# Attention plus gated layer on one core: the mask tables of the opening built in fewer steps, and the check of the two counts moved behind the last minimum

## The chip, the cores and the metric

The kernel runs on one core of a Trainium2 chip. The metric is device time in microseconds (us) of one execution. Engines are named as in the profile: PE multiplies matrices, PEld loads its weights, DVE, ACT and POOL work on vectors, SP issues most transfers; ACT can issue transfers too, in a queue of its own.

## The reference

Four batches of eight heads, 768 positions, head size 64. A query sees a key if the key is one of the first `n_global` (8) positions or lies 0 to `n_local`-1 (95) positions behind it. The two counts are inputs (int64), so the mask is made on the chip. The attention's output goes through a gated layer with 512 inputs and 1536 hidden units.

```
rel = pos[:, None] - pos[None, :]
is_global = pos[None, :] < int(n_global)
is_local = (rel >= 0) & (rel < int(n_local))
keep = is_global | is_local
dist = where(is_global & ~is_local, n_local, abs(rel))
scores = scale * q @ k.T - slopes[h] * dist        # kept places
scores = where(keep, scores, -1e9)
a = exp(scores - max); a = a / (sum(a) + 1e-9); x = a @ v
out = (sigmoid(x @ w_gate) * (x @ w_val)) @ w_out
```

## The kernel before

The tokens are cut into 8 blocks of 384 (three tiles of 128). A block's attention goes by pairs of heads: four pairs, three tiles each. A tile's window has 256 keys: 96 before it, 32 slots for the global keys, and its own 128. For a tile the kernel computes scores on PE (L368), adds a distance table and takes the row's minimum on DVE (L401, `tensor_tensor_reduce`), the exponential on ACT (L414), transposes on PE (L447), and the product with v on PE (L497). The gated layer follows with 12 slices of hidden units (L559 into the layer, L599 out of it).

Block 0's attention runs alone, as an opening; from then on the attention of a block is woven into the gated layer of the block before. During block 0 the weights, which arrive as 64-bit numbers, are also rebuilt as pairs of 32-bit halves (L193 and L200 on ACT, L209 on DVE, L230 on ACT, L181 on POOL).

The opening needs the distance tables. `n_local` and `n_global` come as two transfers on SP's queue (L77), ahead of the queries and keys (L296, L304, L305). DVE makes 32-bit floats of their low and high words and joins them (`nf`, L81 to L84); `build_tables` (L109) forms distances (`dist` for 256 keys, `dist0` for the 128 keys of a sequence's first tile) from index ramps that POOL writes (L113 to L117), and `build_pair` (L152) scales them by a head's slope: on DVE for the first pair, on POOL for the other three. `tab` are the 256-wide tables, `tabs` the 128-wide ones for first tiles.

The tables hold only for counts within bounds (`n_local` 1 to 97, `n_global` 0 to 32). The kernel tests that, and whether a row had no key at all, in one `flag` (L758 to L768): four comparisons of `nf`, one of the largest minimum. At the end every engine loads the flag (L844) and branches (L845): flag 0 ends the program, flag 1 runs a general version of the whole (not run with these inputs). The program's end also waits for the last stores of the output (`ost` to `out`, L625 on SP, L619 on ACT).

A scheduler orders the instructions of each engine; `issue_after` only adds an order between two of them. Within an engine they run in that order. The pools of the main part are closed at L748 (`inner.close()`); the pool `gpool`, opened after that (L750), lies on their memory, among it that of `ost`, so a tile in it may be written only when whoever used that memory before is done.

Of the kernel before, what the change touches and what calls it, by code (L numbers as in the profile page):

```python
# [16 lines left out]
ALU = mybir.AluOpType  # L17
# [3 lines left out]
P = 128  # L21
PREV = 96
GLOB = 32
SLOT = GLOB + P
WIN = PREV + SLOT
NEG = 1.0e30


@with_exitstack
def attn_moe_kernel(ctx, tc, qT, kT, v, n_global, n_local, wg, wv, wo, out, B, H, S, D):  # L30
    nc = tc.nc
    DM = H * D
    NC = DM // P
# [23 lines left out]
    spool = inner.enter_context(tc.tile_pool(name="spool", bufs=2))  # L57
# [5 lines left out]
    def issue_after(later, earlier):  # L63
        tc.add_manual_dep(
            later.ins,
            earlier.ins.name,
            mybir.DependencyInfo(mybir.DependencyClass.NoSync, mybir.DependencyReason.DATA),
            reason="issue order",
        )


    nf = cpool.tile([P, 2], F32, name="nf")


    words = cpool.tile([P, 2, 2], I32, name="words")
    for k, src in enumerate((n_local, n_global)):
        nc.sync.dma_start(  # L77
            words[:, k], src.bitcast(I32)[0:2].rearrange("(a b) -> a b", a=1).to_broadcast([P, 2])
        )
    wf = cpool.tile([P, 3, 2], F32, name="wf")  # L80
    nc.vector.tensor_copy(wf[:, 0:2].rearrange("p w k -> p k w"), words)  # L81
    nc.vector.tensor_scalar(wf[:, 2], wf[:, 0], 0.0, None, op0=ALU.is_lt)
    nc.vector.tensor_tensor(wf[:, 2], wf[:, 2], wf[:, 1], op=ALU.add)
    nc.vector.scalar_tensor_tensor(nf, wf[:, 2], 2.0 ** 32, wf[:, 0], op0=ALU.mult, op1=ALU.add)  # L84
    ident = cpool.tile([P, P], F32, name="ident")
    warm = cpool.tile([P, 1], F32, name="warm")
    nc.vector.memset(warm, 0.0)
# [18 lines left out]
    tabs = [cpool.tile([P, WIN], BF16, name=f"tab{h}") for h in range(H)]  # L106
    tabs0 = [cpool.tile([P, P], BF16, name=f"tabs{h}") for h in range(H)]
    nms = cpool.tile([P, 2 * (B * NTB * NPAIR)], F32, name="nms")
    def build_tables():  # L109

        nl, ng = nf[:, 0:1], nf[:, 1:2]
        reli = spool.tile([P, WIN], I32, name="pT", tag="pT", bufs=PTB)
        nc.gpsimd.iota(reli[:, 0:PREV], pattern=[[-1, PREV]], base=PREV, channel_multiplier=1)  # L113
        nc.gpsimd.iota(reli[:, PREV:PREV + GLOB], pattern=[[1, GLOB]], base=0, channel_multiplier=0)
        nc.gpsimd.iota(reli[:, PREV + GLOB:WIN], pattern=[[-1, P]], base=0, channel_multiplier=1)
        coli = mpool.tile([P, P], I32, name="work", tag="work", bufs=WORKB)
        nc.gpsimd.iota(coli, pattern=[[1, P]], base=0, channel_multiplier=0)  # L117
        rel = spool.tile([P, WIN], F32, name="pT", tag="pT", bufs=PTB)
        nc.vector.tensor_copy(rel, reli)
        col = mpool.tile([P, 2, P], F32, name="work", tag="work", bufs=WORKB)  # L120
        nc.vector.tensor_copy(col[:, 0], coli)
        loc = spool.tile([P, WIN], F32, name="pT", tag="pT", bufs=PTB)
        pen = mpool.tile([P, 2, P], F32, name="work", tag="work", bufs=WORKB)
        cur = slice(PREV + GLOB, WIN)
        kg, only, both = col[:, 0], col[:, 1], pen[:, 0]
        nc.vector.tensor_scalar(loc, rel, 0.0, None, op0=ALU.is_ge)
        nc.vector.tensor_scalar(kg, kg, ng, None, op0=ALU.is_lt)
        nc.vector.scalar_tensor_tensor(loc, rel, nl, loc, op0=ALU.is_lt, op1=ALU.mult)
        nc.vector.tensor_tensor(rel, rel, loc, op=ALU.mult)
        dist = wraw.tile([P, WIN], BF16, name="dist", bufs=1)  # L130
        dist0 = wraw.tile([P, P], BF16, name="dist0", bufs=1)

        nc.vector.tensor_tensor(only, kg, loc[:, cur], op=ALU.is_gt)
        nc.vector.tensor_tensor(both, kg, loc[:, cur], op=ALU.max)
        nc.vector.scalar_tensor_tensor(only, only, nl, rel[:, cur], op0=ALU.mult, op1=ALU.add)
        nc.vector.tensor_scalar(both, both, 1.0, NEG, op0=ALU.subtract, op1=ALU.mult)
        nc.vector.tensor_tensor(dist0, both, only, op=ALU.subtract)
        build_pair(0, True, (dist, dist0))

        gsl = slice(PREV, PREV + GLOB)  # L140
        nc.vector.tensor_copy(loc[:, gsl], kg[:, 0:GLOB])
        nc.vector.tensor_scalar(rel[:, gsl], kg[:, 0:GLOB], nl, None, op0=ALU.mult)
        nc.vector.tensor_scalar(loc, loc, 1.0, NEG, op0=ALU.subtract, op1=ALU.mult)
        nc.vector.tensor_tensor(dist, loc, rel, op=ALU.subtract)
        return dist, dist0

    built = set()
    last_min = []
# [3 lines left out]
    def build_pair(s, zero, dist):  # L152
        if (s, zero) in built:
            return
        built.add((s, zero))
        for h in (2 * s, 2 * s + 1):
            eng = nc.gpsimd if s else nc.vector
            eng.tensor_scalar((tabs0 if zero else tabs)[h], dist[zero], slopes[h] / SCALE, None, op0=ALU.mult)


    w1h = [wpool.tile([P, 2, NC, P], F32R, name=f"w1h{f}") for f in range(NF)]
# [192 lines left out]
    def scores(bi, s, t):  # L354
# [542 lines left out]
```

## Time and profile before

| | us |
|---|---|
| median of three runs | 739.73 (738.4 to 740.57) |
| the profiled execution | 739.84 |
| its span, first to last instruction | 738.1 |
| PE busy in the span | 722.8 (98%) |
| DVE, ACT, POOL busy | 474.7, 410.8, 228.2 |

All times in the sections below are from the start of that span. A row of the timeline gives start, duration, engine, line of the code, operation, what it writes and reads, and in brackets how long the engine had been idle and what ended that. Rows of engines with a q (SPq, ACTq, DVEq) are what an engine's sequencer does: issuing a transfer, loading a flag, branching, waiting for a semaphore.

### The profile page before, as it was taken

What the parts mean: (1) busy time and instruction counts of PE and PEld (TensorE: products, weight loads), DVE (VectorE), ACT (ScalarE), POOL (GpSimd) and SP (SyncE); (2) the same over time, 40 slices, a digit from 0 to 9 for tenths busy, and PEclk for the clock granted to TensorE, in tenths of its full rate; (3) what the DMA queues carried; (4) which work ended last, traced back from release to release, by engine and by line L of the source; (5) the groups of instructions that cost most, each with busy time, mean ns of one, the idle gap of its engine ahead of it and who ended that gap; (6) DMA issues with size and microseconds to landing.
All of it is one profiled execution on the core that took longest, in us unless ns stands there. A gap on an engine that the chain in (4) does not pass through costs nothing. (4 is left out here: it accounts for less than half of the span.)

```text
span 738.1 us, 12514 instructions
## 1 busy us (share of the span) xinstructions
PE 722.8 (98%) x4403; PEld 655.9 (89%) x4403; DVE 474.7 (64%) x1279; ACT 410.8 (56%) x938; POOL 228.2 (31%) x238
## 2 busy tenths in 40 slices
PE   8999999999999999999999999999999999999996
PEld 5758788989889999999999999999999999999995
DVE  6765577577877877776777777666787867321111
ACT  4787686656555555565456655555555664332222
POOL 5437366323222323232232323213232231221222
PEclk8999999999999999999999999999999999999999
DMA  8688573524455342442435442353435234010001
GB/s 256 182 256 273 175 211 101 134 56 88 101 89 152 83 110 68 91 113 58 87 84 112 118 102 69 52 133 75 96 78 112 72 44 86 16 44 1 1 0 46
DMA packets 136868, 74.28 MB, mean 101 GB/s; under 512 B 87136, under 2 KB 129120, under 8 KB 136800
## 3 DMA queue, kind: packets, MB, share of 16 engines
q1 hardware_dynamic: 136656, 73.17, 40.0%
q8 instruction: 36, 0.59, 0.4%
q14 instruction: 32, 0.26, 0.1%
q10 hardware_dynamic: 144, 0.26, 0.1%
HBM read 49.81 MB, written 6.29 MB: 76 GB/s over the span
## 5 line engine op out<-in xcount | busy, mean ns | idle before, releaser
L181 POOL TENSOR_TENSOR w2l<-w2f,w2h 128x512 fp32r<-128x512 f32 x89 | 120.3, 1351 | 361.9 <-ACT w2h L212 354.8
L559 PE MATMUL ps_g<-xh,w1l 128*128 128x384 f32 x384 | 132.1, 344 | 1.1 <-ACT work L567 1.1
L559 PE MATMUL ps_u<-xh,w1l 128*128 128x384 f32 x384 | 130.8, 341 | 0.1
L559 PE MATMUL ps_g<-xl,w1h 128*128 128x384 f32 x384 | 129.6, 338 | 0.2 <-DVE xl L540 0.2
L559 PE MATMUL ps_g<-xh,w1h 128*128 128x384 f32 x384 | 129.6, 337 | 0.0
L559 PE MATMUL ps_u<-xl,w1h 128*128 128x384 f32 x384 | 129.3, 337 | 0.0
L559 PE MATMUL ps_u<-xh,w1h 128*128 128x384 f32 x384 | 129.1, 336 | 0.0
L576 DVE SCALAR_TENSOR_TENSOR work<-work,ps_u 128x384 f32<-128x384 f32 x90 | 49.7, 552 | 123.4 <-PE ps_u L559 122.6
L579 ACT ACTIVATE hh<-work 128x384 fp32r<-128x384 f32 x90 | 46.9, 521 | 128.4 <-DVE work L576 128.3
L414 ACT ACTIVATE work<-work,nms 128x256 f32<-128x256 f32 (+1 forms) x192 | 92.0, 480 | 30.0 <-DVE nms L401 29.5
L599 PE MATMUL ps_o<-w2l,hh 128*128 128x512 f32 x267 | 104.7, 392 | 1.8 <-POOL w2l L181 1.8
L599 PE MATMUL ps_o<-w2h,hh 128*128 128x512 f32 x267 | 104.1, 390 | 0.0
L599 PE MATMUL ps_o<-w2h,hl 128*128 128x512 f32 x267 | 103.6, 389 | 0.0
L181 DVE TENSOR_TENSOR hl<-work,hh 128x384 fp32r<-128x384 f32 x90 | 78.8, 875 | 25.4 <-ACT hh L579 25.3
L212 ACT ACTIVATE w2h<-w2f 128x512 fp32r<-128x512 f32 x89 | 56.0, 630 | 55.1 <-PE ps_o L599 54.3
L559 PEld LDWEIGHTS ps_g<-xh,w1l 128*128 128x128 f32 x384 | 72.3, 188 | 5.3 <-issue 2.1
L559 PEld LDWEIGHTS ps_u<-xh,w1l 128*128 128x128 f32 x384 | 72.1, 188 | 4.0 <-issue 1.0
L559 PEld LDWEIGHTS ps_g<-xl,w1h 128*128 128x128 f32 x384 | 72.2, 188 | 2.8 <-issue 1.0
L559 PEld LDWEIGHTS ps_u<-xl,w1h 128*128 128x128 f32 x384 | 72.2, 188 | 1.0
L559 PEld LDWEIGHTS ps_g<-xh,w1h 128*128 128x128 f32 x384 | 72.2, 188 | 0.6 <-issue 0.3
L462 DVE COPY halves<-work 128x512 int16<-128x512 int16 (+1 forms) x144 | 62.8, 478 | 15.0 <-DMA turned<-halves 13.4
L559 PEld LDWEIGHTS ps_u<-xh,w1h 128*128 128x128 f32 x384 | 72.2, 188 | 0.0
(131 smaller groups left out, 1160.6 us busy)
## 6 DMA issues: line engine op xcount, KB each, us to landing
qr<-in_qT SPq DMA_DIRECT2D x56, 192.0 KB, 3.4
kr<-in_kT SPq DMA_DIRECT2D x32, 192.0 KB, 2.7
v<-in_v SPq DMA_DIRECT2D x32, 192.0 KB, 3.4
raw<-in_w_gate SPq DMA_DIRECT2D x12, 512.0 KB, 5.2
raw<-in_w_val SPq DMA_DIRECT2D x12, 512.0 KB, 6.1
raw<-in_w_out SPq DMA_DIRECT2D x12, 512.0 KB, 3.8
out<-ost SPq DMA_DIRECT2D x23, 256.0 KB, 2.1
v<-in_v SPq DMA_DIRECT2D x16, 144.0 KB, 3.7
```

What stands on the lines that cost most here:

```text
L181: eng.tensor_tensor(out, a, b, op=ALU.subtract)
L212: ins = nc.scalar.activation(hi, w, AF.Copy)
L414: ins = nc.scalar.activation(sb[:, j, :w], sb[:, j, :w], AF.Exp, scale=-1.0, bias=nm[:, j:j + 1], accum_out=sm[:, j:j + 1])
L462: nc.vector.tensor_copy(dst, words[:, :, :, h])
L559: nc.tensor.matmul(ps[:, :n], wt[f][:, i, c], xt[:, c, :n], start=(k == 0), stop=(k == 3 * NC - 1))
L576: nc.vector.scalar_tensor_tensor(a[:, :n], a[:, :n], 1.0, pss[1][:, :n], op0=ALU.add, op1=ALU.mult)
L579: nc.scalar.activation(hh[:, :n], a[:, :n], AF.Copy)
L599: ins = nc.tensor.matmul(outs[bi][t], ht[:, t * P:(t + 1) * P], wt, start=(f == 0 and k == 0), stop=(f == NF - 1 and k == len(parts) - 1),)
```

## The change

The two counts are joined into one array (`counts`, the host stacks them as they are), and one transfer on ACT's queue brings them. The tables are made from the low words alone (`low`): the ramps are written so that one product gives a huge number where a place is ruled out, and maxima and minima combine them, straight from the integers. The sign of the slope moves into the scaling. The join of low and high words, with the four comparisons that use it, moves behind the main loop, into `gpool`, and is placed in order behind the last minimum. Lines of the new kernel have other numbers; L139 is its L158, L382 its L401, L831 its L844.

```
-    for k, src in enumerate((n_local, n_global)):
-        nc.sync.dma_start(
-            words[:, k], src.bitcast(I32)[0:2].rearrange("(a b) -> a b", a=1).to_broadcast([P, 2])
-        )
-    wf = cpool.tile([P, 3, 2], F32, name="wf")
-    nc.vector.tensor_copy(wf[:, 0:2].rearrange("p w k -> p k w"), words)
-    nc.vector.tensor_scalar(wf[:, 2], wf[:, 0], 0.0, None, op0=ALU.is_lt)
-    nc.vector.tensor_tensor(wf[:, 2], wf[:, 2], wf[:, 1], op=ALU.add)
-    nc.vector.scalar_tensor_tensor(nf, wf[:, 2], 2.0 ** 32, wf[:, 0], op0=ALU.mult, op1=ALU.add)
+    nc.scalar.dma_start(words.rearrange("p k w -> p (k w)"), counts.bitcast(I32).rearrange("(a b) -> a b", a=1).to_broadcast([P, 4]))
+    low = cpool.tile([P, 2], F32, name="low")
...
+        nc.vector.tensor_scalar(off, reli, 0.0, NEG, op0=ALU.is_lt, op1=ALU.mult)
+        nc.vector.tensor_tensor(rel, reli, off, op=ALU.max)
+        nc.vector.tensor_copy(low, words[:, :, 0])
...
+        nc.vector.tensor_scalar(off, rel, nl, NEG, op0=ALU.is_ge, op1=ALU.mult)
+        nc.vector.tensor_scalar(dist0, col, ng, NEG, op0=ALU.is_ge, op1=ALU.mult)
+        nc.vector.tensor_tensor(dist, rel, off, op=ALU.max)
+        nc.vector.tensor_scalar(dist0, dist0, nl, None, op0=ALU.max)
+        nc.vector.tensor_copy(dist[:, gsl], dist0[:, 0:GLOB])
+        nc.vector.tensor_tensor(dist0, dist0, dist[:, cur], op=ALU.min)
         build_pair(0, True, (dist, dist0))
...
-            eng.tensor_scalar((tabs0 if zero else tabs)[h], dist[zero], slopes[h] / SCALE, None, op0=ALU.mult)
+            eng.tensor_scalar((tabs0 if zero else tabs)[h], dist[zero], -slopes[h] / SCALE, None, op0=ALU.mult)
...
     late["pool"] = gpool
+    nf = gpool.tile([P, 2], F32, name="nf")
+    wf = gpool.tile([P, 3, 2], F32, name="wf")
+    issue_after(nc.vector.tensor_copy(wf[:, 0:2].rearrange("p w k -> p k w"), words), last_min[-1])
+    nc.vector.tensor_scalar(wf[:, 2], wf[:, 0], 0.0, None, op0=ALU.is_lt)
+    nc.vector.tensor_tensor(wf[:, 2], wf[:, 2], wf[:, 1], op=ALU.add)
+    nc.vector.scalar_tensor_tensor(nf, wf[:, 2], 2.0 ** 32, wf[:, 0], op0=ALU.mult, op1=ALU.add)
```

The places where the order moves follow. First DVE in the opening. Before, from the arrival of `words` to the first minimum's tables:

```order
L81 CAST wf<-words 128x2x2
L82 TENSOR_SCALAR wf<-wf 128x2
L83 TENSOR_TENSOR wf<-wf 128x2
L84 SCALAR_TENSOR_TENSOR nf<-wf 128x2
L127 TENSOR_SCALAR work<-work,nf 128x128
L128 SCALAR_TENSOR_TENSOR pT<-pT,nf 128x256
L766 TENSOR_SCALAR top<-nf 1x1 x4
...
L137 TENSOR_TENSOR dist_216<-work 128x128
L144 TENSOR_TENSOR dist<-pT 128x256
L158 TENSOR_SCALAR tabs_129<-dist_216 128x128
```

Now, on DVE, from `low` on (two steps, L114 and L115, stand ahead and need no count):

```order
L116 CAST low<-words 128x2
L119 TENSOR_SCALAR work<-work,low 128x256
L120 TENSOR_SCALAR dist_204<-work,low 128x128
L121 TENSOR_TENSOR dist<-work 128x256
L122 TENSOR_SCALAR dist_204<-dist_204,low 128x128
L123 COPY dist<-dist_204 128x32
L124 TENSOR_TENSOR dist_204<-dist_204,dist 128x128
L139 TENSOR_SCALAR tab_115<-dist 128x256
L139 TENSOR_SCALAR tab_116<-dist 128x256
L139 TENSOR_SCALAR tabs_123<-dist_204 128x128
L139 TENSOR_SCALAR tabs_124<-dist_204 128x128
```

Between the arrival of the counts and the first table there were twenty instructions; now there are seven.

Second, POOL's tables for the other three pairs. Before (`tabs_131` and `tabs_132` are the first-tile tables of pair 1, `tab_123` and on the wide ones):

```order
L158 TENSOR_SCALAR tabs_131<-dist_216 128x128
L158 TENSOR_SCALAR tabs_132<-dist_216 128x128
...
L158 TENSOR_SCALAR tabs_136<-dist_216 128x128
L158 TENSOR_SCALAR tab_123<-dist 128x256
L158 TENSOR_SCALAR tab_124<-dist 128x256
```

Now, on POOL (`tab_117` is the wide table of pair 1's first head, `tabs_125` its first-tile table):

```order
L139 TENSOR_SCALAR tab_117<-dist 128x256
L139 TENSOR_SCALAR tab_118<-dist 128x256
...
L139 TENSOR_SCALAR tab_121<-dist 128x256
L139 TENSOR_SCALAR tabs_125<-dist_204 128x128
L139 TENSOR_SCALAR tabs_126<-dist_204 128x128
```

Five wide tables now stand ahead of the first-tile table that pair 1 needs first.

Third, DVE at the end of the program, with what each instruction waits for. Before, behind the last minimum's blocks (the flag was complete some 25 rows earlier, at L768):

```order
L622 TENSOR_SCALAR ost<-ps_o_7680 128x512 [waits DMAHW1_49,DMAHW0_49,PE_49]
L617 TENSOR_SCALAR ost<-ps_o_7681 128x256 [waits DMAHW2_49,PE_49]
L844 TENSOR_LOAD flag [waits DVE_49]
L845 COMPARE_AND_BRANCH
```

Now, on DVE, the same place (`DMAHW` are semaphores of transfers; the values waited for on 2, 3 and 4 are those that the last three stores of `ost` set, `DMAHW4` being ACT's, the very last):

```order
L598 TENSOR_SCALAR ost<-ps_o_7666 128x256 [waits DMAHW1_49,PE_49]
L735 CAST wf<-words 128x2x2 [waits DMAHW3_49,DMAHW4_49,DMAHW2_49,DMAHW7_49,Activation_49,Pool_49]
L736 TENSOR_SCALAR wf<-wf 128x2 [waits DVE_49]
L737 TENSOR_TENSOR wf<-wf 128x2 [waits DVE_49]
L738 SCALAR_TENSOR_TENSOR nf<-wf 128x2 [waits DVE_49]
L753 TENSOR_SCALAR top<-nf 1x1 [waits DVE_49]
L753 TENSOR_SCALAR top<-nf 1x1 x3
L755 TENSOR_REDUCE flag<-top 1x1 [waits DVE_49]
L831 TENSOR_LOAD flag [waits DVE_49]
L832 COMPARE_AND_BRANCH
```

Nine instructions moved from the opening and from the main loop to behind the last store, and the flag's load on all engines stands behind them.

## Rows read from the trace of the kernel before

**Rows 1.** The page: busy time of PE, PEld, DVE, ACT and POOL.

```profile
PE 722.8 (98%) x4403; PEld 655.9 (89%) x4403; DVE 474.7 (64%) x1279; ACT 410.8 (56%) x938; POOL 228.2 (31%) x238
```

**Rows 2.** Windows: length, busy of PE, PEld, DVE, ACT, POOL, clock, DMA share, GB/s.

```profile
11.00:21.00 10.00, 10.00 (x55) 6.56 (x51) 5.14 (x19) 8.10 (x24) 5.92 (x8) 0.51 0.88 313
...
22.00:30.00 8.00, 7.71 (x74) 4.96 (x73) 6.37 (x30) 5.24 (x21) 6.05 (x12) 1.00 0.85 259
...
40.00:100.00 60.00, 59.21 (x319) 43.96 (x318) 38.27 (x100) 45.69 (x96) 27.93 (x57) 1.00 0.75 232
100.00:728.00 628.00, 624.12 (x3805) 582.99 (x3805) 408.87 (x1074) 340.36 (x775) 180.37 (x141) 1.00 0.35 80
```

**Rows 3.** Timeline of DVE, opening.

```profile
4.77 0.17 DVE L81 CAST wf<-words 128x4 f32<-128x4 int32 x1 [2.37 <-DMA words<-in_n_global]
...
5.57 0.29 DVE L127 TENSOR_SCALAR work<-work,nf 128x128 f32<-128x128 f32 x1
...
6.17 0.32 DVE L766 TENSOR_SCALAR top<-nf 1x1 f32<-1x1 f32 x4
...
8.18 0.41 DVE L144 TENSOR_TENSOR dist<-pT 128x256 bf16<-128x256 f32 x1
8.52 0.40 DVE L158 TENSOR_SCALAR tabs<-dist 128x128 bf16<-128x128 bf16 x2
...
9.12 0.27 DVE L401 CUSTOM_DVE_ANT_0 work<-ps_s,tabs 128x128 f32<-128x128 f32 x1
```

**Rows 4.** Timeline of SP, opening: issues of transfers.

```profile
0.85 0.39 SPq L77 DMA_DIRECT2D words<-in_n_local  x1
...
1.76 0.43 SPq L296 DMA_DIRECT2D qr<-in_qT  x1
```

**Rows 5.** Transfers issued from 0 to 9 us: count, KB each, us to landing.

```profile
words<-in_n_local SPq DMA_DIRECT2D x1, 1.0 KB, 2.6
words<-in_n_global SPq DMA_DIRECT2D x1, 1.0 KB, 3.4
```

**Rows 6.** Timeline of PE, opening.

```profile
6.17 0.34 PE L368 MATMUL ps_g<-kr,qr 64*128 64x128 f32 x1 [1.12 <-DMA kr<-in_kT]
...
9.66 0.48 PE L368 MATMUL ps_g<-kr,qr 64*128 64x256 f32 x1 [1.48 <-DVE nms L401]
...
10.66 0.37 PE L368 MATMUL ps_o<-kr,qr 64*128 64x128 f32 x1
...
21.48 0.37 PE L368 MATMUL ps_g<-kr,qr 64*128 64x128 f32 x1
...
27.05 0.37 PE L368 MATMUL ps_o<-kr,qr 64*128 64x128 f32 x1
```

**Rows 7.** Timeline of ACT, opening.

```profile
14.55 1.10 ACT L193 ACTIVATE bits<-raw 128x1024 int32<-128x1024 uint32 x1
15.55 1.11 ACT L200 ACTIVATE top<-raw 128x1024 f16<-128x1024 bf16 x1
...
20.05 1.06 ACT L230 ACTIVATE w1h<-bits 128x1024 fp32r<-128x1024 f32 x1
...
22.36 0.40 ACT L414 ACTIVATE work<-work,nms 128x128 f32<-128x128 f32 x1 [1.25 <-DVE nms L401]
```

**Rows 8.** Timeline of POOL, tables of pairs 1 to 3.

```profile
8.34 3.66 POOL L158 TENSOR_SCALAR tabs<-dist 128x128 bf16<-128x128 bf16 x6 [6.26 <-DVE dist L137]
12.08 5.14 POOL L158 TENSOR_SCALAR tab<-dist 128x256 bf16<-128x256 bf16 x6
```

**Rows 9.** Line L845, SP waiting for stores: count, ns min/median/max, first to last.

```profile
L845 SPq EVENT_SEMAPHORE  x8: 17/17/17, 733.6 to 736.7; - x8
```

**Rows 10.** Line L768, the flag's reduction: count, ns min/median/max, first to last.

```profile
L768 DVE TENSOR_REDUCE flag<-top x1: 147/147/147, 655.8 to 655.8; 1x1 int32<-1x5 f32 x1
```

**Rows 11.** The chain that ended last: its end (start, us, what).

```profile
732.65 0.37 DVEq L844
...
733.74 0.06 DVE top L846
```

More of the change, by code (lines that the diff above doesn't have):

```diff
@@ L29, in attn_moe_kernel @@
 @with_exitstack
-def attn_moe_kernel(ctx, tc, qT, kT, v, n_global, n_local, wg, wv, wo, out, B, H, S, D):
+def attn_moe_kernel(ctx, tc, qT, kT, v, counts, wg, wv, wo, out, B, H, S, D):
     nc = tc.nc
@@ L69, in issue_after @@
         )
-    nf = cpool.tile([P, 2], F32, name="nf")
     words = cpool.tile([P, 2, 2], I32, name="words")
-    for k, src in enumerate((n_local, n_global)):
-        nc.sync.dma_start(
-            words[:, k], src.bitcast(I32)[0:2].rearrange("(a b) -> a b", a=1).to_broadcast([P, 2])
-        )
-    wf = cpool.tile([P, 3, 2], F32, name="wf")
-    nc.vector.tensor_copy(wf[:, 0:2].rearrange("p w k -> p k w"), words)
-    nc.vector.tensor_scalar(wf[:, 2], wf[:, 0], 0.0, None, op0=ALU.is_lt)
-    nc.vector.tensor_tensor(wf[:, 2], wf[:, 2], wf[:, 1], op=ALU.add)
-    nc.vector.scalar_tensor_tensor(nf, wf[:, 2], 2.0 ** 32, wf[:, 0], op0=ALU.mult, op1=ALU.add)
+    nc.scalar.dma_start(words.rearrange("p k w -> p (k w)"), counts.bitcast(I32).rearrange("(a b) -> a b", a=1).to_broadcast([P, 4]))
+    low = cpool.tile([P, 2], F32, name="low")
     ident = cpool.tile([P, P], F32, name="ident")
@@ L109, in build_tables @@
     def build_tables():
-        nl, ng = nf[:, 0:1], nf[:, 1:2]
+        nl, ng = low[:, 0:1], low[:, 1:2]
+        cur, gsl = slice(PREV + GLOB, WIN), slice(PREV, PREV + GLOB)
         reli = spool.tile([P, WIN], I32, name="pT", tag="pT", bufs=PTB)
         nc.gpsimd.iota(reli[:, 0:PREV], pattern=[[-1, PREV]], base=PREV, channel_multiplier=1)
-        nc.gpsimd.iota(reli[:, PREV:PREV + GLOB], pattern=[[1, GLOB]], base=0, channel_multiplier=0)
-        nc.gpsimd.iota(reli[:, PREV + GLOB:WIN], pattern=[[-1, P]], base=0, channel_multiplier=1)
@@ L116, in build_tables @@
[L116 to L129, printed above, removed]
+        nc.gpsimd.iota(reli[:, gsl], pattern=[[0, GLOB]], base=-1, channel_multiplier=0)
+        nc.gpsimd.iota(reli[:, cur], pattern=[[-1, P]], base=0, channel_multiplier=1)
@@ L130, in build_tables @@
+        col = mpool.tile([P, P], I32, name="work", tag="work", bufs=WORKB)
+        nc.gpsimd.iota(col, pattern=[[1, P]], base=0, channel_multiplier=0)
+        far = mpool.tile([P, 2, WIN], F32, name="work", tag="work", bufs=WORKB)
+        rel, off = far[:, 0], far[:, 1]
+        nc.vector.tensor_scalar(off, reli, 0.0, NEG, op0=ALU.is_lt, op1=ALU.mult)
+        nc.vector.tensor_tensor(rel, reli, off, op=ALU.max)
+        nc.vector.tensor_copy(low, words[:, :, 0])
         dist = wraw.tile([P, WIN], BF16, name="dist", bufs=1)
@@ L131, in build_tables @@
         dist0 = wraw.tile([P, P], BF16, name="dist0", bufs=1)
[L133 to L137, printed above, removed]
-        build_pair(0, True, (dist, dist0))
-        gsl = slice(PREV, PREV + GLOB)
@@ L141, in build_tables @@
[L141 to L144, printed above, removed]
+        nc.vector.tensor_scalar(off, rel, nl, NEG, op0=ALU.is_ge, op1=ALU.mult)
+        nc.vector.tensor_scalar(dist0, col, ng, NEG, op0=ALU.is_ge, op1=ALU.mult)
+        nc.vector.tensor_tensor(dist, rel, off, op=ALU.max)
@@ L880 @@
         "v": _np.ascontiguousarray(v.transpose(0, 2, 1, 3)).reshape(B * S, H * D),
-        "n_global": _np.asarray(inputs["n_global"]).reshape(1),
-        "n_local": _np.asarray(inputs["n_local"]).reshape(1),
+        "counts": _np.stack([inputs["n_local"], inputs["n_global"]]),
         "w_gate": _slices(inputs["moe_w_gate"]),
```

## The prediction, made before the changed kernel ran

> **What bounds the kernel now.** I read the page first: PE is busy 722.8 of 738.1 us [rows 1]. Then the windows: from 100 to 728 us PE lacks only 3.9 us of being always busy, from 40 to 100 us only 0.8 [rows 2]. So most of the run is PE's own work, which the change leaves alone; it can win or lose only at the two ends, and what the opening gains arrives at the end as long as the stretch from 40 to 100 us can follow.
>
> In the opening PE waits. It starts on the scores at 6.17, when the keys land, and is stopped again for 1.48 us until 9.66 by the first minima [rows 6]. DVE meanwhile waits 2.37 us for the second list of counts, starts at 4.77 and builds tables until the first minimum at 9.12 [rows 3]. Behind that the granted clock is at its lower level (0.51 over 11 to 21, so 1.2 GHz); PE is called busy all ten microseconds, and pair 2 starts at 21.48. At the upper level (2.4 GHz) pair 2 takes 27.05 - 21.48 = 5.6 us, while pair 1, begun at 10.66, held PE 10.8 us before pair 2's start [rows 2, 6].
>
> At the end DVE's last instruction is at 733.74, but SP waits for the stores until 736.7, and the span closes at 738.1: 1.4 us of leaving behind the last store [rows 9, 11].
>
> **The opening, step by step.** *Counts.* The one transfer is issued by ACT at about 0.8, as SP's first was at 0.85, and lands 2.6 to 3.4 us later [rows 4, 5]: DVE starts on it at 3.5 to 4.3, I take 3.9. SP loses two issues, so queries and keys go out 1.76 - 0.85 = 0.9 us sooner, and the first scores can start at 5.3 [rows 4, 6].
>
> *Tables.* Four tiny dependent steps took 5.57 - 4.77 = 0.8, so 0.2 each; four comparisons that don't depend on each other 0.32; a dependent product of two 256-wide tiles 0.34 (8.18 to 8.52); the four scalings 0.60 (8.52 to 9.12) [rows 3]. The new chain: `low` 0.2, the two threshold steps 0.4, the 256-wide maximum 0.34, a 128-wide maximum 0.2, the copy 0.2, the minimum 0.2, the scalings 0.6: 2.1 in place of 9.12 - 4.77 = 4.35. The two steps ahead of `low` run while DVE sat idle. No row has an operation from integers to a 16-bit table; if each of the seven cost as much as the 256-wide product's 0.4 us, the chain were 3.4, if all were tiny 2.0. The first minimum then stands at 6.0 (5.5 to 7.7): 3.1 us sooner, held back neither by the scores (5.3 plus half a microsecond) nor by the exponential table that ACT now loads 0.4 us later.
>
> *What is late next.* PE had work until its stop, 9.66 - 1.48 = 8.2 [rows 6]; begun 0.9 sooner that ends at 7.3, when the minima of the first tile are done. The third tile's scores start there rather than at 9.66 (2.4 us sooner), and the stop is gone. POOL now writes five wide tables ahead of pair 1's first-tile table: five by 5.14 / 6 = 0.86 and one by 0.61 [rows 8] from about 5.3 make 10.2, where DVE wants it at about 10. That costs 0.2 us, up to 1 if POOL starts late.
>
> *The raw weights.* ACT's L193 needs weights that SP issues only 0.9 us sooner: 14.55 becomes about 13.5. In the new order ACT does L193 and L200 (2.1 from the first's start to the second's end), a copy and pair 1's last two exponentials (0.4 to 0.5 each; the narrower exponential took 0.40) and L230 (1.1), and only then pair 2's first exponential [rows 7]: 13.5 + 2.1 + 1.3 + 1.1 = 18.0, where before it was at 22.36. That is 4.4 us, if PE is at the upper clock level; if PE falls to the lower level as before, it sets the pace and the gain stays at the 3.1 of the first minimum.
>
> On the clock the rows show the lower level from about 11 us on, behind the stop of 1.48 us, and that pairs 2 and 3 held the upper one with PE busy 7.71 of 8 us [rows 2, 6]. I take the upper level as likelier, since between 5.3 and 12 us PE now has work of that density, with a stop of perhaps half a microsecond for pair 1's keys.
>
> *Behind it.* The gated layer's start moves by the same 4.4; PE was busy 59.2 of the 60 us to 100, so the shift is kept, less what the weights' rebuilding can't follow: 0 to 1 us, I take 0.
>
> One page speaks against these numbers. The Trainium skill, DMA: Bandwidth & Descriptors, Issuing engines are not separate DMA queues, says that transfers of all issuers run on the same 16 engines and interleave, so another issuer saves issue time alone. By it the counts now share those engines with a 192 KB load instead of standing ahead of it; at the 313 GB/s of the stretch from 11 us that is 0.6 us, the first minimum would gain 2.5, and the forecast, in which ACT's work ahead of L193 then ends 0.2 us late, 4.2 in place of 4.4. No run here shows the two loads together yet.
>
> **The end, step by step.** The join of the words now waits for the last store, which SP too saw done at 736.7 [rows 9]. Behind it stand four dependent tiny steps (0.8), four comparisons (0.3) [rows 3] and the reduction (0.15, with its hand-over 0.2) [rows 10]: 1.3. Then the flag's load, which no longer stands early, the branch and DVE's last instruction: from 732.65 to 733.80, 1.15 [rows 11]. Together 2.5, all of it on the path, since SP's wait is over by then and the 1.4 us of leaving follow as before. Bounds: 2.0, if SP, which has no last instruction to do, leaves 0.5 sooner than DVE; 3.4, if five engines loading the flag at once take twice as long. Taking the nine instructions out of DVE's earlier work gains nothing further: what lay on a path there is already in the opening's chain.
>
> **The sum.** The profiled execution took 739.84 (span 738.1 and 1.7 around it), 0.1 above the median of 739.73. 739.84 - 4.4 + 2.5 = 737.9. Its own range, with 3.5 to 5.3 for the opening and 2.0 to 3.4 for the end: 736.5 to 739.7.
>
> **Rivals.** *B, the clock falls all the same.* DVE, ACT and POOL keep their pace, PE runs pair 1 at half speed again; opening 3.1, end 2.5: 739.2. For it: the order in the opening has new stops (keys of pair 1, ACT's two microseconds of weights). Against: the stop of 1.48 us is gone.
>
> *C, the weights decide.* Everything behind the opening hangs on raw weights that come only 0.9 us sooner: the first minimum's 3.1 us turn into idle time ahead of L193 and the layer's start moves by 0.9 alone; with the end's 2.5 the run is slower: 739.84 - 0.9 + 2.5 = 741.4. It decides if ACT's L193 is what everything up to the layer waits for in a line. For it: ACT was busy 8.1 of 10 us there, the highest share of the three [rows 2]. Against: it had 1.25 us of idle time ahead of 22.36 [rows 7], and other work can go ahead of L193.
>
> *D, the end costs nothing.* The comparison runs while the last store is under way, as its new place behind the last minimum suggests: 739.84 - 4.4 = 735.4. Against: the order shows the wait for that very store.
>
> *E, the clock gives the whole stretch back.* If pair 1 too took 5.6 us from 8.3 (10.66 less 2.4), pair 2 would start at 13.9, 7.6 us sooner: 739.84 - 7.6 + 2.5 = 734.7. Against: L193 cannot start before 13.5. The Trainium skill, TensorE: Matmul & The Clock Gate, Part 1: The HAM clock gate, says that the slow level is what idleness brings and that activity alone lifts it; by that rule closing PE's stop of 1.48 us gives this case. The low level behind the stop agrees with it; that PE is called busy from 11 to 21 us and stays at the low level does not.
>
> **How the numbers follow.** The forecast has 0.42, B 0.25, C 0.18, D 0.04, E 0.11. A measurement of this kernel can tell about 0.3%, 2.2 us: faster is below 737.5, slower above 741.9. Faster: four tenths of the forecast's range, D, E and a little of B, together 0.34. Slower: four tenths of C, where the end costs near its upper bound, and a little of B: 0.10. Within: 0.56. The range goes from 735.6, which leaves out most of E, to 741.5, which leaves out the upper half of C.
>
> **What would show it.** First minimum at about 6.0 and pair 2's first exponential at about 18; no lower clock between 11 and 21 (if it is there, B). `wf` behind the last store, and about 3.9 us from that store's landing to the end in place of 1.4. If the layer's start moves by 1 us or less, C; if DVE's last instruction still comes before SP's last wait, D.

## The result, and the profile after

| | before | after |
|---|---|---|
| median, us (range, executions) | 739.05 (734.83 to 740.57, 8) | 745.07 (742.24 to 745.9, 8) |
| the profiled execution | 739.84 | 744.83 |
| its span | 738.1 | 742.9 |

The change made the kernel slower: the ratio is 1.0088, 95% interval 1.0062 to 1.0114, some 6.5 us (6.0 by the medians). The prediction was 737.9, with a range from 735.6 to 741.5: the time lies outside it, and it moved the other way.

One fact about the kernel before is needed for every comparison below. In the later runs, 72 more of its executions were timed: 12 had a mean granted clock of 0.991 to 0.993 and took 738.7 to 740.7 us, the other 60 had 0.997 to 1.0 and took 734.7 to 737.6. The profiled execution that the prediction was worked out from (mean clock 0.991) is of the rarer kind. (Of the eight executions in the table five took 738.4 us or more; their clocks are not on record, so how rare the kind is comes from the later runs alone.) The changed kernel's eight have 0.990 to 0.997.

Where did the 5.0 us between the two profiled executions go? I followed the same instruction of each trace through the span. The changed kernel is 1.2 us ahead at 110 us, and 2.8 us behind at 722 us; at the end of the span it is 4.9 behind, and the time outside the span is 0.1 longer (1.89 against 1.78). So: opening -1.15, the long stretch +4.02, the end +2.01, outside +0.11.

**The opening.** DVE in the changed kernel, as in [rows 3]:

```profile
3.86 0.17 DVE L116 CAST low<-words 128x2 f32<-128x2 int32 x1 [1.46 <-DMA words<-in_counts]
4.06 0.35 DVE L119 TENSOR_SCALAR work<-work,low 128x256 f32<-128x256 f32 x1
...
5.49 0.55 DVE L139 TENSOR_SCALAR tab<-dist 128x256 bf16<-128x256 bf16 x2
...
6.50 0.29 DVE L382 CUSTOM_DVE_ANT_0 work<-ps_s,tabs 128x128 f32<-128x128 f32 x1
```

The first minimum stands at 6.50 where it was at 9.12. DVE started on the counts at 3.86, as the sum had it; the half microsecond to the forecast 6.0 lies in the four scalings, 1.0 (5.49 to 6.50) in place of 0.6. ACT, as in [rows 7]: the raw weights' first step and pair 2's first exponential:

```profile
13.60 1.15 ACT L174 ACTIVATE bits<-raw 128x1024 int32<-128x1024 uint32 x1 [0.63 <-DMA raw<-in_w_val]
...
18.11 0.39 ACT L395 ACTIVATE work<-work,nms 128x128 f32<-128x128 f32 x1
```

Up to here the chain comes as it was forecast (13.5 and 18.0). Then PE, as in [rows 6] (L349 are scores, L478 the product with v, L540 the gated layer):

```profile
16.12 0.34 PE L349 MATMUL ps_g<-kr,qr 64*128 64x128 f32 x1 [1.29 <-DMA kr<-in_kT]
...
21.97 0.50 PE L349 MATMUL ps_o<-kr,qr 64*128 64x128 f32 x1 [2.61 <-DMA kr<-in_kT]
...
22.68 2.40 PE L478 MATMUL ps_v<-pT,v 128*64 128x128 f32 x20
...
29.16 1.31 PE L478 MATMUL ps_v<-pT,v 128*64 128x128 f32 x20
...
30.60 0.42 PE L540 MATMUL ps_g<-xh,w1l 128*128 128x384 f32 x1
```

PE stops twice for keys, 1.29 us for pair 2's and 2.61 for pair 3's; behind the second stop the twenty products of pair 1 with v take 2.40 us. In the trace of before these twenty take 1.31 and stand ahead of pair 3's scores (27.05 in [rows 6]), and the layer starts at 30.69, ahead of pair 2's products with v (31.57), which in the changed kernel stand in front of it (29.16):

```profile
25.44 1.31 PE L497 MATMUL ps_v<-pT,v 128*64 128x128 f32 x20
...
30.69 0.42 PE L559 MATMUL ps_g<-xh,w1l 128*128 128x384 f32 x1
...
31.57 1.31 PE L497 MATMUL ps_v<-pT,v 128*64 128x128 f32 x20
```

So the layer's start moved by 0.1 us, not by 4.4. Since the work in front of it is not the same, a later point compares better: the first slice of the layer that DVE multiplies (L576, now L557) comes 1.2 us sooner. Before, then after:

```profile
93.27 0.56 DVE L576 SCALAR_TENSOR_TENSOR work<-work,ps_u 128x384 f32<-128x384 f32 x1 [0.51 <-PE ps_u L559]
```

```profile
92.08 0.56 DVE L557 SCALAR_TENSOR_TENSOR work<-work,ps_u 128x384 f32<-128x384 f32 x1 [0.49 <-PE ps_u L540]
```

Windows of the changed kernel, columns as in [rows 2]; the first and the two last answer to rows shown there:

```profile
11.00:21.00 10.00, 6.21 (x57) 3.82 (x52) 6.93 (x29) 9.23 (x29) 6.86 (x14) 1.00 1.05 339
...
22.00:26.00 4.00, 4.00 (x37) 3.60 (x38) 0.79 (x6) 1.13 (x5) 0.00 (x0) 0.57 0.78 253
...
40.00:100.00 60.00, 59.43 (x320) 44.50 (x319) 37.17 (x98) 46.58 (x98) 27.73 (x57) 1.00 0.71 220
100.00:728.00 628.00, 625.66 (x3785) 583.42 (x3784) 404.93 (x1072) 338.83 (x771) 176.20 (x138) 1.00 0.35 80
```

The clock is at its upper level from 11 to 21 us, where it had been at the lower, but PE is now busy 6.21 of the 10 us and the transfers fill their engines (share 1.05). The clock falls behind the stop for keys, from 22 us on (0.57).

**The long stretch.** The last two windows look like before: PE hardly idles. But the same work takes longer. DVE's L576 (now L557) comes once per slice of hidden units; where PE alone sets the pace, its starts are one slice apart. First before, then after:

```profile
678.21 0.55 DVE L576 SCALAR_TENSOR_TENSOR work<-work,ps_u 128x384 f32<-128x384 f32 x1 [4.50 <-PE ps_u L559]
684.41 0.56 DVE L576 SCALAR_TENSOR_TENSOR work<-work,ps_u 128x384 f32<-128x384 f32 x1 [4.50 <-PE ps_u L559]
```

```profile
680.61 0.55 DVE L557 SCALAR_TENSOR_TENSOR work<-work,ps_u 128x384 f32<-128x384 f32 x1 [4.56 <-PE ps_u L540]
686.88 0.55 DVE L557 SCALAR_TENSOR_TENSOR work<-work,ps_u 128x384 f32<-128x384 f32 x1 [4.56 <-PE ps_u L540]
```

A slice takes 6.20 us before and 6.27 after (medians of the pairs of 6.2 to 6.35 us from 640 to 728 us, the others having more or less work between them: 6.207 and 6.267, 0.97% more) at a granted clock of 1.00 in both. Single multiplications show it too. Four in a row of the changed kernel:

```profile
690.76 0.34 PE L540 MATMUL ps_u<-xh,w1l 128*128 128x384 f32 x1
690.94 0.34 PE L540 MATMUL ps_u<-xl,w1h 128*128 128x384 f32 x1
691.12 0.34 PE L540 MATMUL ps_u<-xh,w1h 128*128 128x384 f32 x1
691.29 0.34 PE L540 MATMUL ps_u<-xh,w1l 128*128 128x384 f32 x1
```

Their starts are 0.17 to 0.18 us apart. In nanoseconds, the trace of before has 173 to 175 nearly throughout; after has 173 to 176 and, about each fifth time, 181 or 182.

**The end.** DVE behind the last stores (ACT issues the last one at 735.96), and SP's waits for the stores as in [rows 9]:

```profile
738.25 0.17 DVE L735 CAST wf<-words 128x4 f32<-128x4 int32 x1 [2.74 <-DMA out<-ost]
...
739.05 0.32 DVE L753 TENSOR_SCALAR top<-nf 1x1 f32<-1x1 f32 x4
739.41 0.15 DVE L755 TENSOR_REDUCE flag<-top 1x1 int32<-1x5 f32 x1
740.92 0.06 DVE L833 MEMSET top<- 1x1 f32 x1 [1.37 <-issue]
```

```profile
L832 SPq EVENT_SEMAPHORE  x8: 17/17/17, 740.7 to 741.2; - x8
```

From where DVE sees the store landed (738.25) to the span's end (742.9) it is 4.7 us; before, from where SP saw it (736.7) to 738.1, it was 1.4. But the last store landed 2.1 us behind its issue, where it had been 3.4, so the end costs 2.0: from PE's last end to the span's end it is 7.9 us (735.05 to 742.9) against 5.9 (732.18 to 738.1).

### The profile page after: what moved, and what is told of

Read it like the earlier page. It is cut to its first block, busy times and chain, and to the rows that moved or that the text cites. A ratio compares the mean times of both kernels' runs of the same rounds, so it can differ in the third digit from the quotient of the medians.

```text
span 742.9 us, 12506 instructions
## 1 busy us (share of the span) xinstructions
PE 725.2 (98%) x4403; PEld 659.1 (89%) x4403; DVE 469.5 (63%) x1273; ACT 410.9 (55%) x938; POOL 227.5 (31%) x238
## 4 chain that ended last, share of the span: by engine, by line
PE 77%; DMA 2%; DVE 2%; ACT 1%; POOL 1%; issue 0%; DVEq 0%; SPq 0%; POOLq 0%; ACTq 0%
PE ps_u L540 23%; PE ps_g L540 23%; PE ps_o L580 23%; PE ps_s L363 4%; PE ps_t L478 2%; PE ps_v L478 2%; DMA turned<-halves 2%; DMA qr<-in_qT 0%; DVE halves L443 0%; POOL w1l L162 0%; DVE ks L162 0%; DMA out<-ost 0%; POOL qs L162 0%; ACT qs L321 0%; DVE work L557 0%
## 5 line engine op out<-in xcount | busy, mean ns | idle before, releaser
L540 PE MATMUL ps_g<-xh,w1l 128*128 128x384 f32 x384 | 132.4, 345 | 1.0 <-ACT work L548 1.0
L557 DVE SCALAR_TENSOR_TENSOR work<-work,ps_u 128x384 f32<-128x384 f32 x90 | 49.6, 552 | 129.7 <-PE ps_u L540 128.8
L540 PE MATMUL ps_u<-xh,w1l 128*128 128x384 f32 x384 | 131.4, 342 | 0.1
L540 PE MATMUL ps_g<-xl,w1h 128*128 128x384 f32 x384 | 130.1, 339 | 0.2 <-DVE xl L521 0.2
L540 PE MATMUL ps_g<-xh,w1h 128*128 128x384 f32 x384 | 130.0, 339 | 0.0
L540 PE MATMUL ps_u<-xl,w1h 128*128 128x384 f32 x384 | 129.9, 338 | 0.0
L540 PE MATMUL ps_u<-xh,w1h 128*128 128x384 f32 x384 | 129.6, 337 | 0.0
L560 ACT ACTIVATE hh<-work 128x384 fp32r<-128x384 f32 x90 | 46.9, 521 | 125.7 <-DVE work L557 125.7
L162 DVE TENSOR_TENSOR hl<-work,hh 128x384 fp32r<-128x384 f32 x90 | 77.3, 859 | 25.8 <-ACT hh L560 25.7
L193 ACT ACTIVATE w2h<-w2f 128x512 fp32r<-128x512 f32 x89 | 56.1, 630 | 58.1 <-PE ps_o L580 57.0
L540 PEld LDWEIGHTS ps_g<-xh,w1l 128*128 128x128 f32 x384 | 72.2, 188 | 5.5 <-issue 2.3
L540 PEld LDWEIGHTS ps_u<-xh,w1l 128*128 128x128 f32 x384 | 72.1, 188 | 4.1 <-issue 1.0
L540 PEld LDWEIGHTS ps_g<-xl,w1h 128*128 128x128 f32 x384 | 72.2, 188 | 2.9 <-issue 1.0
L540 PEld LDWEIGHTS ps_u<-xl,w1h 128*128 128x128 f32 x384 | 72.1, 188 | 1.2
L540 PEld LDWEIGHTS ps_g<-xh,w1h 128*128 128x128 f32 x384 | 72.2, 188 | 0.7 <-issue 0.3
L540 PEld LDWEIGHTS ps_u<-xh,w1h 128*128 128x128 f32 x384 | 72.1, 188 | 0.0
L414 DVE TENSOR_SCALAR work<-work,rc 128x256 f32<-128x256 f32 (+1 forms) x168 | 67.9, 443 | 1.9
```

The source lines that it names most:

```text
L162: eng.tensor_tensor(out, a, b, op=ALU.subtract)
L193: ins = nc.scalar.activation(hi, w, AF.Copy)
L414: nc.vector.tensor_scalar(sb[:, j, :w], sb[:, j, :w], rc[:, j:j + 1], None, op0=ALU.mult)
L540: nc.tensor.matmul(ps[:, :n], wt[f][:, i, c], xt[:, c, :n], start=(k == 0), stop=(k == 3 * NC - 1))
L557: nc.vector.scalar_tensor_tensor(a[:, :n], a[:, :n], 1.0, pss[1][:, :n], op0=ALU.add, op1=ALU.mult)
L560: nc.scalar.activation(hh[:, :n], a[:, :n], AF.Copy)
```

## The experiments

Ratios are to the kernel before, timed beside each on the same chip, with 95% intervals.

**The long stretch: place.** The change takes `nf` and `wf` out of the pool of constants and puts `low` in. Every tile has a whole multiple of 32 bytes per partition there, so all tiles behind it lie 32 bytes lower; the weights `w1h` and `w1l`, ahead of it, stay. Five kernels moved tiles and nothing else of the work: in their traces each engine has the same instructions in the same order as in the kernel they are made from.

e1, the changed kernel, padded so that every later tile lies as before:

```
     low = cpool.tile([P, 2], F32, name="low")
+    pad = cpool.tile([P, 8], F32, name="pad")
```

> The changed kernel with 32 unused bytes per partition added to the pool of constants, so that every later tile lies where it lay before the change. Theory P (place): the layer's multiplications run 0.97% slower in the changed kernel (6.266 against 6.206 us a slice from 640 to 728 us) because the tiles behind the constants lie 32 bytes lower; put back, the 4.3 us lost between 45 and 730 us come back: 745.1 - 4.3 = 740.8, slice at 6.206. Rival R (the run or the chip, not the place: a clock, instruction reading): 745.1 again, slice at 6.266.

e2, the kernel before, padded:

```
+    pad = cpool.tile([P, 8], F32, name="pad")
     ident = cpool.tile([P, P], F32, name="ident")
```

> The kernel before with the same 32 unused bytes per partition, and nothing else, so all tiles behind the constants lie 32 bytes higher. Theory P: if what counts is the place modulo 64 bytes, it gets the slow slices of the changed kernel: 739.1 + 4.3 = 743.4, slice near 6.266. Rival R: 739.1, slice 6.206.

e4, the kernel before, pads around the layer's inputs:

```
+    xpool.tile([P, 8], F32, name="pada")
     xall = [xpool.tile([P, 2 * NC * NB], F32R, name=name) for name in ("xh", "xl")]
+    xpool.tile([P, 8], F32, name="padb")
```

> The kernel before with 32 unused bytes ahead of xh and 32 behind xl: xh and xl, the tiles that stream through the layer's first multiplications, lie 32 bytes higher, all tiles behind them 64 bytes higher. If the place of xh and xl alone decides: slow slices, 743.4. If it is another tile's place modulo 64: 739.1.

p1 is e4 without its first pad, p2 has the one pad ahead of `w1h` instead (one profiled execution each):

> The kernel before with 32 unused bytes behind xl: xh and xl stay, hh, hl, w2h, w2l and all else behind them lie 32 bytes higher. If the place of xh and xl alone decides, the slice from 640 to 728 us takes 6.206 us, as before. If that of the later tiles does (or as well): 6.25 or more.

> The kernel before with 32 unused bytes ahead of the weights w1h and w1l, so that they and all tiles behind them, xh and xl too, lie 32 bytes higher. If what counts is how xh and xl lie against the weights (modulo 64 bytes), nothing changes: slice at 6.206. If it is the place of xh and xl in itself: 6.25 to 6.28.

Measured, with the bytes by which tiles lie higher (+) or lower (-) than before; the slice is the median from 640 to 728 us, worked out as above:

| kernel | w1h, w1l | xh, xl | tiles behind | slice, us | ratio to before |
|---|---|---|---|---|---|
| before | 0 | 0 | 0 | 6.207 | 1 |
| after | 0 | -32 | -32 | 6.267 | 1.0088 (1.0062 to 1.0114) |
| e1 | 0 | 0 | 0 | 6.207 | 1.0054 (1.0033 to 1.0076) |
| e2 | 0 | +32 | +32 | 6.252 | 1.0049 (1.0030 to 1.0068) |
| e4 | 0 | +32 | +64 | 6.280 | 1.0083 (1.0056 to 1.0109) |
| p1 | 0 | 0 | +32 | 6.320 | not known (one execution: 739.80 us) |
| p2 | +32 | +32 | +32 | 6.207 | not known (one execution: 735.54 us) |

In e2 the pairs fall into two groups, 6.245 to 6.252 and 6.291 to 6.295, and 6.252 is the median of both together. The rows of e1, p1 and p2, in this order, from which a slice is read:

```profile
678.43 0.55 DVE L558 SCALAR_TENSOR_TENSOR work<-work,ps_u 128x384 f32<-128x384 f32 x1 [4.50 <-PE ps_u L541]
684.64 0.56 DVE L558 SCALAR_TENSOR_TENSOR work<-work,ps_u 128x384 f32<-128x384 f32 x1 [4.50 <-PE ps_u L541]
```

```profile
678.13 0.55 DVE L577 SCALAR_TENSOR_TENSOR work<-work,ps_u 128x384 f32<-128x384 f32 x1 [4.58 <-PE ps_u L560]
684.45 0.55 DVE L577 SCALAR_TENSOR_TENSOR work<-work,ps_u 128x384 f32<-128x384 f32 x1 [4.62 <-PE ps_u L560]
```

```profile
673.64 0.55 DVE L577 SCALAR_TENSOR_TENSOR work<-work,ps_u 128x384 f32<-128x384 f32 x1 [4.50 <-PE ps_u L560]
679.85 0.55 DVE L577 SCALAR_TENSOR_TENSOR work<-work,ps_u 128x384 f32<-128x384 f32 x1 [4.50 <-PE ps_u L560]
```

With the places of before, the changed kernel keeps the pace of before: e1 stands 0.2 us behind it at 265 us and 0.2 at 722. With nothing but places moved, the kernel before gets 0.7% to 1.8% slower slices. Clock and instructions are excluded: the profiled executions of e2 and p1 had a mean clock of 1.0, and the seven other kernels below, whose tiles lie as in before or, behind the weights, 64 bytes higher, have 6.207 each, with openings of their own. What counts is how tiles lie against each other: with all moved by 32 bytes (p2) nothing changes, nor with those behind the weights moved by 64; in each of the four slow kernels some tiles have moved by 32 bytes against others. It isn't `xh` and `xl` alone, as I had thought possible: in p1 these and the weights lie as before, and the slice is the slowest. Which pairs of tiles disturb each other, and how, stays open.

**The end.** e3 is e1 with the join's tiles among the constants, so it needs no store (all tiles behind the constants lie 64 bytes higher than before). x1 is the kernel before, with a second join behind the main loop, as in the changed kernel.

```
e3:
     pad = cpool.tile([P, 8], F32, name="pad")
+    nf = cpool.tile([P, 2], F32, name="nf")
+    wf = cpool.tile([P, 3, 2], F32, name="wf")
...
-    nf = gpool.tile([P, 2], F32, name="nf")
-    wf = gpool.tile([P, 3, 2], F32, name="wf")
x1:
     late["pool"] = gpool
+    nf = gpool.tile([P, 2], F32, name="nf")
+    wf = gpool.tile([P, 3, 2], F32, name="wf")
+    issue_after(nc.vector.tensor_copy(wf[:, 0:2].rearrange("p w k -> p k w"), words), last_min[-1])
...
```

> The changed kernel with the tiles of the 64-bit join (nf, wf) back among the constants and 32 unused bytes, so tiles lie 64 bytes above those of before and the join can run right behind the last minimum. Theory: the join behind the last store costs 3.3 us at the end as its profile shows (landing to end 4.7 us against 1.4): 3.3 less than the padded changed kernel, 737.5 if that comes to 740.8. Rival: the store's faster landing (2.1 against 3.4 us) was part of the same thing, so only 2.0 comes back: 738.8. If place counts by itself beyond 64 bytes, it lies elsewhere.

> The kernel before, with a second join of the 64-bit words behind the main loop, from which the flag's comparisons are made, as in the changed kernel; opening and places untouched. It prices the end by itself: from PE's last multiplication to the end 7.9 us as in the changed kernel, in place of 5.9, so 2.0 more: 738.1 beside 736.1 of before. If the quick landing of the last store (2.1 us) in the changed kernel's profile was luck, 3.3 more: 739.4. If the wait is hidden: the same as before.

e3 took 738.41 (1.0021, 1.0004 to 1.0038), e1 741.47: 3.1 us by the medians. x1 took 738.11 beside 736.10 (1.0032, 1.0014 to 1.0051): 2.0. The profiles of e1 and e3 agree with the 2.0: from PE's last end to the span's end they have 7.9 and 5.9 us. The rest of the 3.1 lies in front: with the same order on PE the profiled e1 stopped 3.78 us for pair 3's keys and e3 1.70. (x1 also takes the four comparisons out of DVE's opening.) SP's waits and DVE's last instruction in e3, whose last store is issued at 730.41:

```profile
L833 SPq EVENT_SEMAPHORE  x8: 17/17/17, 730.9 to 734.0; - x8
```

```profile
731.05 0.06 DVE L834 MEMSET top<- 1x1 f32 x1 [1.09 <-issue]
```

DVE is done 3 us before SP sees the store, as before the change; the span ends at 735.4. In x1 the join begins at 731.30 and the span ends at 736.0, again 4.7 later; its last store landed in 2.1 us too. The end costs 2.0 us, and it is the place of two small tiles in the pool on reused memory that costs them. The two don't lie on the stores' own bytes: in the program as built `nf` and `wf` are where `kr` was, and the order shows them waiting for `ost` all the same. The wait comes with the pool.

**The opening: order or bytes.** In e3, place and end are mended, and it is still 1.0021 of before. One of its twelve executions had a mean clock of 1.0, and that one took 735.82 us; the other eleven had 0.991 to 0.997 and took 737.0 to 740.1. Its PE and a window of it:

```profile
20.86 0.34 PE L352 MATMUL ps_o<-kr,qr 64*128 64x128 f32 x1 [1.70 <-DMA kr<-in_kT]
...
21.32 2.40 PE L481 MATMUL ps_v<-pT,v 128*64 128x128 f32 x20
...
29.49 0.42 PE L543 MATMUL ps_g<-xh,w1l 128*128 128x384 f32 x1
```

```profile
21.00:24.00 3.00, 3.00 (x30) 2.84 (x32) 0.79 (x6) 1.13 (x5) 0.44 (x2) 0.53 0.92 310
```

f2 is e3 with one order added on PE: pair 1's products with v ahead of pair 3's first scores (`first_av` holds the last of them). f1 is e3 with one order added on SP: the second slice's raw gate and value weights behind pair 3's keys. f12 has both.

```
f2, in scores:
+                elif (bi, s, t) == (0, NPAIR - 1, 0):
+                    issue_after(ins, first_av[-1])
f1, in conv_load and load_step:
+                if j == 2:
+                    issue_after(ins, keys_at[0, NPAIR - 1])
...
-        nc.sync.dma_start(
+        keys_at[bi, s] = nc.sync.dma_start(
             kslots[:, first:, 0:GLOB],
```

> The kernel of the run with the early join (e3: 738.4, at 1.0021 of before), and one added order: PE multiplies pair 1 with v ahead of pair 3's first scores, as it does in the kernel before. Theory O (order): in the changed kernel PE stops at pair 3's scores until their keys land (1.70 us there, 2.61 in the changed kernel), with 20 multiplications that need no key queued behind them; the clock falls behind that stop, and the layer starts 8.6 us behind pair 3's scores where before it is 3.6. With the order back the multiplications fill the wait: no lower clock from 20 to 25 us, layer's start at 25 to 27 instead of 29.5, time 734 to 736. Rival B (bytes): the transfers set the pace, so the stop only moves and the layer starts at 29 again: 738.

> The early-join kernel (e3), and one added order on SP: the 1 MB of the second slice's raw weights is issued behind pair 3's keys, not ahead of pair 2's values. Theory B (bytes): pair 3's keys, under way for 5 us, land in 3 to 4, PE's stop for them (1.70) is gone or below 0.5, the layer starts at 27 to 28: 736 to 737. Theory O: PE's order is unchanged, so a stop of whatever length stays at pair 3's scores; it falls only by what the keys come sooner. If the second slice's weights then come too late for the layer, the time is 738.4 or more.

> The early-join kernel with both added orders: pair 1's multiplications with v ahead of pair 3's scores, and the second slice's raw weights behind pair 3's keys. If both the order and the bytes held the opening up, this is the fastest: 733 to 735, layer's start at 24.5 to 26. If one of them is enough, the same as the better of the two alone.

f2 took 735.77 (0.9992, 0.9976 to 1.0008), f1 734.62 (0.9988, 0.9976 to 1.0001), f12 735.14 (0.9989, 0.9979 to 0.9999). PE of f2 and its window, then of f1:

```profile
19.41 1.31 PE L484 MATMUL ps_v<-pT,v 128*64 128x128 f32 x20 [0.16 <-DVE pT L437]
...
22.20 0.37 PE L353 MATMUL ps_o<-kr,qr 64*128 64x128 f32 x1
...
27.59 0.42 PE L548 MATMUL ps_g<-xh,w1l 128*128 128x384 f32 x1
```

```profile
21.00:24.00 3.00, 3.00 (x29) 2.04 (x31) 2.00 (x9) 0.82 (x3) 1.49 (x4) 1.00 0.98 351
```

```profile
19.38 0.37 PE L355 MATMUL ps_o<-kr,qr 64*128 64x128 f32 x1
...
26.67 0.42 PE L546 MATMUL ps_g<-xh,w1l 128*128 128x384 f32 x1
```

Each alone takes the stop for pair 3's keys away, and in each the clock stays up: in f2 the products fill the wait, in f1 the keys are there at 19.38 (3.5 us on the way, where e3's took 5.1). Together they bring nothing more: f12's layer starts at 28.38. But against a kernel before whose clock does not fall little is gained. p2, which is the kernel before but for its places, had a mean clock of 0.999; its PE (L369 scores, L560 layer) and window:

```profile
9.64 0.48 PE L369 MATMUL ps_g<-kr,qr 64*128 64x256 f32 x1 [1.47 <-DVE nms L402]
...
26.96 0.42 PE L560 MATMUL ps_g<-xh,w1l 128*128 128x384 f32 x1
```

```profile
11.00:21.00 10.00, 9.17 (x81) 5.89 (x79) 8.43 (x33) 9.51 (x31) 7.68 (x13) 1.00 1.06 350
```

The first minimum is late and the stop of 1.47 us is there, and still the layer starts at 26.96, 3.7 us ahead of the profiled execution of before. In f1 and f2 pair 2's products with v stand in front of the layer's start, in p2 behind it, so again the first slice on DVE compares better. p2, f1 and f2:

```profile
89.60 0.55 DVE L577 SCALAR_TENSOR_TENSOR work<-work,ps_u 128x384 f32<-128x384 f32 x1 [0.54 <-PE ps_u L560]
```

```profile
88.00 0.55 DVE L563 SCALAR_TENSOR_TENSOR work<-work,ps_u 128x384 f32<-128x384 f32 x1 [0.48 <-PE ps_u L546]
```

```profile
88.57 0.55 DVE L565 SCALAR_TENSOR_TENSOR work<-work,ps_u 128x384 f32<-128x384 f32 x1 [0.48 <-PE ps_u L548]
```

So the changed opening, with its stop cured, is 1.6 (f1) or 1.0 us (f2) ahead of p2 there; 1.0 and 0.1 are left at 722 us. The first minimum's 2.6 us shrink on the way. From 11 to 21 us the transfers fill their engines in the changed kernel and in p2 (1.05 and 1.06), and shorter tables do not change what has to be moved; that this is the reason was not tested by itself.

f3 is e3 with the counts at the front of SP's queue; g1 is the kernel before with f1's added order.

```
f3:
-    nc.scalar.dma_start(words.rearrange(
+    nc.sync.dma_start(words.rearrange(
```

> The early-join kernel with the counts' one transfer at the front of SP's queue instead of on ACT's. If the other queue is what sets the opening off (queries and keys 0.45 us sooner, and with them the order that the scheduler chose), the scheduler's order here, with pair 3's keys ahead of pair 2's values on SP, shortens the stop: 736 to 737. If the queue only costs its issue, 0.4 us later than on ACT's: 738.4 to 738.8.

> The kernel before, with the one added order on SP that the changed kernel's opening was given (raw weights of the second slice behind pair 3's keys). If the gain over the early-join kernel came from a fault that the change brought, it does nothing here: 735.5 to 737. If the opening is short of transfers in both, it is 1 to 2 us faster than before: 734 to 735, and the shorter tables of the change are worth nothing beside it.

Both missed on the other side: f3 739.99 (1.0057, 1.0031 to 1.0082), g1 739.49 (1.0062, 1.0040 to 1.0083). In both, the layer starts early (25.91 and 26.39), and the time is lost behind it, where block 1's attention is woven in. PE of g1:

```profile
37.45 0.48 PE L371 MATMUL ps_v<-kr,qr 64*128 64x256 f32 x1 [1.22 <-DVE nms L404]
...
43.72 0.44 PE L562 MATMUL ps_g<-xh,w1l 128*128 128x384 f32 x1 [2.56 <-ACT work L570]
```

p2 has no such stop as 2.56 there; at 60 us g1 is 3.3 us behind p2 and f3 2.7. The scheduler wrote another order in both, on PE from 20 us on in g1 and from 11 us on in f3, far beyond what the edits touch. So these two say nothing clean on how the queue or the bytes act on the whole. f3 does show the counts' way: at the front of SP's queue they took 2.9 us to land, on ACT's queue 3.0 in the changed kernel.

## Why the prediction was wrong, step by step

- **Counts, tables, first minimum: right in kind, half a microsecond late.** 6.50 against 6.0, a gain of 2.6 against 3.1. The counts came as the sum had them (3.86 against 3.9); the scalings were mis-sized, 1.0 against 0.6. By the rule of the Trainium skill, DMA: Bandwidth & Descriptors, Issuing engines are not separate DMA queues, I had worked out a gain of 2.5, with counts that land 0.6 us later because they share the engines. That 2.6 came is luck: the counts took 3.0 us on ACT's queue (3.1 in e3) and 2.9 in f3, ahead of all loads, so by these executions sharing cost 0.1 to 0.2.
- **Scores at 5.3, the third tile's at 7.3, the raw weights at 13.5, pair 2's first exponential at 18.0, upper clock from 11 to 21 us:** measured 5.32, 7.26, 13.60, 18.11, and a granted clock of 1.00. All held.
- **"The gated layer's start moves by the same 4.4 ... so the shift is kept": failed, for two reasons.** First, PE's keys. I followed ACT to pair 2 and took PE to follow; PE's row waits for transfers that were not in the sum. Pair 3's keys came 1.0 us later than before: issued at 16.0 (before 16.4), they were 5.8 us on the way in place of 4.4. The new order had PE stand at them with pair 1's products queued behind; f2 and f1 show that either cure is enough. 4.4 became 1.2. Second, the 4.4 were worked out from an execution whose clock fell, and 60 of 72 later ones kept a mean of 0.997 or more. Against p2, which is the kernel before in all but places and kept 0.999, the opening had 1.0 to 1.6 us to gain (f2, f1), and the changed kernel is 2.5 us behind p2 at its first slice on DVE (92.08 against 89.60).
- **"Most of the run is PE's own work, which the change leaves alone": failed, and it is the largest term.** The change moved every tile behind the constants by 32 bytes, and PE's own work became 0.97% slower: +4.0 us in a term that the sum had at 0. e1, e2 and p2 show it.
- **The end, +2.5 (2.0 to 3.4): right in kind.** 2.0, at the lower bound, as the difference of two misses: 4.7 us behind the store's landing instead of 3.9 (the join and the flag took the 1.3 us of the sum, from there to DVE's last instruction 1.4 in place of 1.15, and from that to the span's end 2.0 in place of 1.4), and a store that landed 1.3 us sooner. That the difference fell on the range's edge is luck.
- **The sum.** 739.84 - 1.15 + 4.02 + 2.01 + 0.11 = 744.83. With the tiles in their old places it would have been 740.8; e1, which has them, took 741.47, just inside the range and still on the wrong side of the forecast.
- **The rivals.** C (741.4, an opening that gains 0.9) had the right size of the opening, and its sign came (the layer's start moved by 0.1), but for the wrong reason: ACT was past L193 and at pair 2 by 18.11, 4.25 us sooner than before, and PE stood at the keys. B had a lower clock, which came, but at 22 us and behind a stop. D and E are out: the wait is there, and the opening gave no 7.6. D's sign misleads: DVE's last instruction (740.92) does come before SP's last wait (741.2), but SP's waits now stand behind the flag. With the rule behind E (the Trainium skill, TensorE: Matmul & The Clock Gate, Part 1: The HAM clock gate, that idleness brings the slow level), these rows agree: the clock falls in the changed kernel, e1 and e3 behind stops of 2.61, 3.78 and 1.70 us, and stays up in f1 and f2, which have no stop for pair 3's keys. But a stop of 1.48 us in the profiled execution of before is followed by the lower level, and the same stop of 1.47 us in p2 is not. What decides between these two stays open.

## What to carry to other kernels

Look at where tiles lie, not only at what is done: an edit that takes a few bytes out of an early pool can slow a stretch it never touches, and one pad tells. Compare a long steady stretch of both traces slice by slice before explaining the ends; and before taking a gain from a low clock, see whether other executions have it. A check moved "off the path" into a pool on reused memory inherits the waits of whoever used that memory last.

The version f12 has the changed tables and puts tiles, join and both orders right; it is faster than the changed kernel, and than the one before by 0.11% (0.01% to 0.21%). f1 has the lower median, 734.62, but its interval reaches 1.0001.

## What the runs showed of the hardware that was not expected

- The time of one slice of 24 multiplications of 384 columns and 9 of 512 was 6.207, 6.252, 6.267, 6.280 or 6.320 us, by the places of the tiles alone, at the same granted clock. In p1 the multiplications of 512 columns are hit as well: most starts are 231 to 236 ns apart, where before has 226 to 229.
- The last store landed 2.1 us behind its issue in the three profiles in which the engines wait for it before they load the flag and branch (after, e1, x1), and 2.6 to 3.7 us in the eleven others, where they branch while it is under way (3.4 in before, e2 and e3). In the eleven, three packets of instructions (kind "instruction" in the profile's list of queues) are moved beside the store; in the three, none until it has landed. Whether these packets are the cause was not tried.
